# Tail groups worked one per period in periods 3 to 6, and layer 1 of group 7 computed with seven block products

## The chip, the cores and the metric

The kernel runs on one core of a Trainium2 chip. Its engines are TensorE (PE, with its weight loads shown apart as PEld), VectorE (DVE), ScalarE (ACT), GpSimd (POOL) and SyncE (SP), which issues nearly all DMAs. The metric is the device time of one execution in microseconds (us), as the median of several runs.

## The reference

```
# q, k, v: [8 batches, 8 heads, 576 positions, 64]
scores = q @ k.T / sqrt(64), kept where 0 <= pos_q - pos_k < 64, else -1e9
attn   = exp(scores - max) / (sum + 1e-9)
x      = attn @ v, heads side by side          # [8, 576, 512]
xn     = (x - mean) / sqrt(var + 1e-6) * g_ln
out    = x + max(xn @ w_ch1, 0) @ w_ch2        # 512 -> 2048 -> 512, float32
```

Each query sees itself and 63 earlier keys; then each row goes through a normalised two-layer network with a residual.

## The kernel before

The rows are worked in nine groups of 512. Groups 0 to 7 are the first 512 positions of batches 0 to 7. Group 8 (`NGRP - 1`, `r` in the main loop) gathers the last 64 positions of all batches: its four blocks of 128 rows are the four "tails", tail `i` holding batches `2i` and `2i + 1`. A block `(g, kb)` of any group passes these steps:

- scores on PE (`s_pe`, L352), exponentials on ACT (`s_exp`, L362), the mask on DVE (`s_mask`, L372);
- values product on PE (`b_pe`, L399); then on DVE `b_rows`: reciprocals of the row sums (L419), the division (L423), statistics (L429, L432);
- `z_step` on POOL: three small instructions and the normalised row in 16 bits (L451 to L457);
- `zt_step`: transposes z into `zT`, by a DMA transpose issued by SP (L477), or for some blocks by four PE transposes (L481) and a copy on ACT (L484).

The loads of a batch (L92, L179) are issued by SP, cast on POOL (L157, L185) and, for q and k, transposed by DMA (L268) or by PE (L279). `part_vB` (L204, L206) copies the cast v, shifted by 64 rows, by DMA. A tail is loaded by `load_tail` (six DMAs: tq, tk, tv, L106 and L109), cast by `cast_tail` on POOL (L118 to L121) and transposed by `t_tail`: tails 0 and 1 on PE (L301, L310), tails 2 and 3 by DMA (L297, L304).

The network is written in `mlp_units(g)`, a list of units. For groups 3 to 7 layer 1 is 16 units (`l1`, L504): four 128x512 matmuls each, and a ReLU on ACT (L508). Group 8 computes layer 1 with seven block products (Strassen's scheme in Winograd's form): each of four chunks `d` has the products 1, 2, 5, 6, 3, 7, 4 in `l1_a` to `l1_e`, four 128x256 matmuls each (L701). Their operands are sums of blocks of the weights (`w1_sums`, tiles `w1S`, L813, on DVE) and differences of blocks of zT (`z_sums`, L830, on DVE); ACT keeps copies of three of them (L713), DVE adds (L716) and takes maxima (L718, a third of them on POOL). Layer 2 of groups 1 to 8 is seven block products of two halves (`stage(n, p)`, L578), 14 units of eight matmuls, with the S sums of the hidden values before them (`s_sums`, L552) and the sums into the rows behind them (L587, L591), both on DVE. Groups 1 to 7 take the products in the order 4, 1, 2, 6, 5, 7, 3, group 8 in the order 1, 2, 6, 5, 7, 4, 3.

The main loop is the plan. Period `g` runs the units of group `g`, and after unit `i` everything that was put in slot `i` with `at(i, f, ...)`: the attention of group `g + 1` (`b` in the code), the loads of group `g + 3`, the casts and transposes of group `g + 2`, and the tails. An engine runs its instructions in the order written, so the slots are the order on every engine, and SP issues DMAs in that order too, each after its own waits. `TAILS = {3: [0], 5: [1], 7: [2, 3]}` says in which period a tail's attention is worked; its loads, casts and transposes lie in the period before. Period 7 also holds the W1 sums, and at its end the first products of group 8.

Of the kernel before, what the change touches and what calls it, by code (L numbers as in the profile page):

```python
# [18 lines left out]
def kernel(  # L19
# [77 lines left out]
    def load_tail(i):  # L97
        tq = p_in.tile([128, H, D], FP32, tag="tq32", name=f"tq32_{i}", bufs=1)
        tk = p_in.tile([128, 2, H, D], FP32, tag="tk32", name=f"tk32_{i}", bufs=1)
        tv = p_in.tile([128, 2, H, D], FP32, tag="tv32", name=f"tv32_{i}", bufs=1)  # L100
        tail32[i] = (tq, tk, tv)
        for n in range(6):
            r = n % 2
            b = 2 * i + r
            if n < 2:
                nc.sync.dma_start(out=tq[64 * r:64 * r + 64], in_=q[b, :, SM:S, :].rearrange("h s d -> s h d"))  # L106
            else:
                t, x = (tk, k) if n < 4 else (tv, v)
                nc.sync.dma_start(out=t[:, r], in_=x[b, :, S - 128:S, :].rearrange("h s d -> s h d"))  # L109
# [181 lines left out]
    def t_tail(i, x):  # L291
        src = tail16[i][x]
        if x == 0:
            tailT[i] = (p_qkt.tile([128, NHP, 128], FP16, tag="tqT", name=f"tqT_{i}", bufs=1),
                        p_qkt.tile([128, 2, NHP, 128], FP16, tag="tkT", name=f"tkT_{i}", bufs=1))
            if i >= 2:
                nc.sync.dma_start_transpose(out=tailT[i][0], in_=src[:, :, :].rearrange("p h d -> p (h d)"))  # L297
                return
# [3 lines left out]
        else:  # L302
            if i >= 2:
# [167 lines left out]
    def zt_step(g, kb, eng="act"):  # L471
# [4 lines left out]
        if XZ <= g and not ((kb == 3 and g in (2, 3, 5)) or (g, kb) == (3, 2)):  # L476
            nc.sync.dma_start_transpose(out=zT[g][:, :, 128 * kb:128 * kb + 128], in_=z)  # L477
            return
# [16 lines left out]
    def mlp_units(g, split=0, three=False, seven=True):  # L495
# [3 lines left out]
        units = []  # L499

# [55 lines left out]
        def product(n, p):  # L556
# [10 lines left out]
            if p == 0 and n in (1, 2 if last else 4, 5):  # L567
# [31 lines left out]
        def stage(n, p):  # L599
# [25 lines left out]
            elif n == 7:  # L625
                post_both("A", 2)
                store(2)
                store(3)
            elif n == 4:
                post("B", 2, 0)  # L630
                if last:
                    store_rest(2, slice(0, 256), None)
            elif n == 3:
# [41 lines left out]
        def l1_product(n, d):  # L675
# [12 lines left out]
            if n == 1:  # L688
                pool, tag = (ps_mm, "mm") if d == 2 else (ps_s, "sc")
                lbank[("A", d)] = pool.tile([128, 2, 256], FP32, tag=tag, name=f"lA_{d}")  # L690
            elif n == 2:
                lbank[("B", d)] = ps_t.tile([128, 2, 256], FP32, tag="t0", name=f"lB_{d}")
            elif n == 5:
                if d % 2:
                    lbank[("C", d)] = ps_t.tile([128, 2, 256], FP32, tag="t1", name=f"lC_{d}")
                else:
                    lbank[("C", d)] = ps_x.tile([128, 4, 256], FP32, tag="xps", name=f"lC_{d}")[:, 0:2]
# [85 lines left out]

        halves = [(half, i) for half in range(2) for i in range(split // 2)]
# [20 lines left out]
    def w1_sums(*which):  # L805
        wv = w1g[:, :, :].rearrange("p (a k) (i e m) -> p a k i e m", a=2, e=2, m=128)
        a11, a12, a21, a22 = (wv[:, b, :, :, a, :] for a, b in ((0, 0), (0, 1), (1, 0), (1, 1)))
        for n in which:
            w1S[n] = p_in.tile([128, NKC // 2, NHC // 2, 128], FP16, tag=f"qk32_{n % 2}", name=f"w1S{n}")
            o = w1S[n][:, :, :, :]  # L810
            x, y, op = {1: (a21, a22, ALU.add), 2: (w1S.get(1), a11, ALU.subtract),
                        3: (a11, a21, ALU.subtract), 4: (a12, w1S.get(2), ALU.subtract)}[n]
            nc.vector.tensor_tensor(out=o, in0=x, in1=y, op=op)  # L813
# [130 lines left out]
    def begin_last():  # L944
        nonlocal rest
        rest, _ = mlp_units(NGRP - 1)

    rest = None
    TAILS = {3: [0], 5: [1], 7: [2, 3]}
    for g in range(NGRP):  # L950
        if g == NGRP - 1:
            for _ in rest:
                pass
            break
        units, s_sums = mlp_units(g, (8, 16, 16)[g] if g < 3 else 0, g == 0, g > 0)
# [159 lines left out]
        elif g > 1 and b < B:  # L1115
            tail = TAILS.get(g)
# [6 lines left out]
            if tail:  # L1123
                r, i = NGRP - 1, tail[0]
                at(2, s_pe, r, i, False, "t")
                at(4, s_exp, r, i, 0)
                at(5, s_exp, r, i, 1)
                at(5, s_mask, r, i)
                at(7, b_pe, b, 1)
                at(7, b_pe, r, i, "t")  # L1130
                at(7, s_mm, b, 3)
                at(7, b_rows, b, 1)
                at(7, z_step, b, 1)
                at(8, s_mask, b, 3)
                at(8, b_rows, r, i)
                at(9, z_step, r, i)
                at(12, b_pe, b, 2)
                at(12, b_pe, b, 3, "sc")
                at(16, zt_step, r, i)
            else:  # L1140
                at(2, s_pe, b, 3, False, "t")
                at(4, s_exp, b, 3, 0)
                at(5, s_exp, b, 3, 1)
                at(5, s_mask, b, 3)
                at(7, b_pe, b, 1)
                at(7, b_pe, b, 2, "t")
                at(7, b_pe, b, 3, "sc")
                at(7, b_rows, b, 1)
                at(7, z_step, b, 1)
            if g + 2 < B:  # L1150
                at(5, alloc_qkT, g + 2)
                at(5, after_mask, *((NGRP - 1, tail[0]) if tail else (b, 3)))
# [3 lines left out]
            for j, i in ((2, 12), (3, 19)):  # L1156
                at(i, b_rows, b, j)
                at(i, z_step, b, j)
            for j in range(4):
                at((2, 14, 18, {3: 25, 5: 25}.get(b, 23))[j], zt_step, b, j)  # L1160
        for n, i in enumerate(TAILS.get(g, ()) if b >= B else ()):
            ts = (13, 13, 17, 22) if n else (1, 2, 5, 11)
            at(ts[0], s_mm, NGRP - 1, i)
            at(ts[1], s_mask, NGRP - 1, i)
            at(ts[2], b_step, NGRP - 1, i)
            at(ts[2], z_step, NGRP - 1, i)
            at(ts[3], zt_step, NGRP - 1, i)
        n = g + 2
        if g > 1 and n < B:
# [5 lines left out]
            at(26, part_vB, n, 0, 4)  # L1175
# [12 lines left out]
        if g > 2:  # L1188
# [60 lines left out]
```

## Time and profile before

Three runs took 299.7 to 299.91 us, median 299.87. The profiled execution took 299.59 us, of which 297.9 us are the span from its first to its last instruction.

| stretch of the span, us | what | PE busy | DVE busy | ACT busy | POOL busy |
|---|---|---|---|---|---|
| 0 to 48.7 | start, period 0's first part | 45.95 | 27.61 | 27.76 | 36.70 |
| 119.4 to 150.16 | period 3, tail 0 worked | 30.76 | 23.64 | 17.37 | 18.98 |
| 150.16 to 180.96 | period 4, tail 1 loaded and transposed | 30.80 | 22.16 | 16.59 | 18.13 |
| 180.96 to 211.76 | period 5, tail 1 worked | 30.80 | 23.63 | 17.37 | 18.75 |
| 211.76 to 240.09 | period 6, tail 2 loaded and transposed | 28.33 | 20.24 | 11.42 | 12.59 |
| 240.09 to 268.3 | period 7, tails 2 and 3 worked | 28.21 | 20.81 | 11.89 | 7.91 |
| 268.3 to 297.9 | rest of group 8, last stores | 25.08 | 22.35 | 8.62 | 6.06 |

How to read the views that follow: in the windows view a line is a stretch, then for each engine its busy time and the count of instructions. In the timeline a line is start, length, engine, line of the kernel, operation, tiles written and read, and in brackets the idle time before it with the instruction that ended it. The chain of work that ended last gives start, length and engine. A line such as L578 is that of the kernel before.

### The profile page before, as it was taken

How to read it: one execution, taken by the hardware profiler on the slowest of the kernel's cores; microseconds unless marked ns; L12 is line 12 of the kernel's file. 1: busy time of each engine (PE TensorE's matmuls, PEld its weight loads, DVE VectorE, ACT ScalarE, POOL GpSimd, SP SyncE). 2: the span in 40 equal slices, each digit the busy share in tenths (PEclk: the TensorE clock that was granted, in tenths of full speed). 3: DMA queues.
4: the chain of work that ended last, by engine and by line, in shares of the span. 5: the costliest groups of instructions: out<-in, count | busy, mean ns of one | idle time of the engine just before them, and what ended most of it. 6: DMA issues, size and time to landing. Idle time of an engine off the chain costs nothing.

```text
span 297.9 us, 7824 instructions
## 1 busy us (share of the span) xinstructions
PE 290.6 (98%) x3187; PEld 206.9 (69%) x3187; DVE 217.9 (73%) x414; ACT 154.4 (52%) x261; POOL 164.2 (55%) x243
## 2 busy tenths in 40 slices
PE   8989999999999999999999999999999999999994
PEld 3657545888888888557854786469646854788883
DVE  2881378899993894489757865698568786789983
ACT  3566647677449526873276428751674056305500
POOL 4688897753850986389518860897048407024300
PEclk9999999999999999999999999999999999999998
DMA  7999999979979999998299999991729497003014
GB/s 189 259 382 339 382 296 284 256 217 300 170 169 302 248 155 223 291 229 143 55 303 257 184 179 274 291 162 40 223 47 183 72 178 194 20 18 143 2 37 107
DMA packets 113223, 58.11 MB, mean 195 GB/s; under 512 B 82593, under 2 KB 104161, under 8 KB 113186
## 3 DMA queue, kind: packets, MB, share of 16 engines
q1 hardware_dynamic: 112752, 57.21, 81.7%
q8 instruction: 25, 0.41, 0.6%
q10 hardware_dynamic: 434, 0.40, 0.4%
q14 instruction: 12, 0.10, 0.1%
HBM read 38.80 MB, written 9.44 MB: 162 GB/s over the span
## 4 chain that ended last, share of the span: by engine, by line
PE 83%; DMA 6%; SPq 5%; POOL 3%; issue 0%; DVE 0%
PE hps L504 24%; PE pA L578 14%; PE hph L645 10%; PE pB L578 10%; PE pC L578 9%; PE xps L399 3%; DMA w2s<-in_moe_w_ch_dram 3%; PE sc L352 3%; DMA wT<-in_moe_w_ch_dram 3%; PE lA L701 2%; PE tp L279 2%; SPq L179 2%; POOL w2s L246 2%; SPq L218 2%; SPq L87 1%; PE lC L701 1%
## 5 line engine op out<-in xcount | busy, mean ns | idle before, releaser
L504 PE MATMUL hps<-zT,w1g 128*128 128x512 f16 x352 | 80.2, 379 | 0.0
L508 ACT ACTIVATE hrT<-hps 128x512 f16<-128x512 f32 x88 | 52.8, 600 | 36.8 <-PE hps L504 33.8
L504 PEld LDWEIGHTS <-w1g 128*128 128x128 f16 x352 | 33.1, 98 | 38.0 <-issue 1.7
L578 PEld LDWEIGHTS <-sS 128*128 128x128 f16 x512 | 49.3, 98 | 5.6
L362 ACT ACTIVATE pt<-sc 128x512 f16<-128x512 f32 x72 | 39.8, 601 | 22.7 <-PE sc L352 22.2
L451 POOL TENSOR_SCALAR rsz<-mvg 128x1 f32<-128x1 f32 x32 | 10.5, 329 | 63.2 <-DVE mvg L432 53.2
L578 PEld LDWEIGHTS <-hrT 128*128 128x128 f16 x384 | 36.7, 98 | 7.0 <-ACT hrT L508 0.8
L645 PE MATMUL hph<-zT,w1g 128*128 128x256 f16 x320 | 37.9, 273 | 0.0
L372 DVE TENSOR_TENSOR pt<-pt,mask 128x1024 f16<-128x1024 f16 x32 | 23.5, 740 | 19.6 <-ACT pt L362 19.6
L157 POOL CAST qk<-qk 128x1024 f16<-128x1024 f32 x29 | 32.5, 1139 | 8.9 <-PE sc L352 5.9
L645 PEld LDWEIGHTS <-w1g 128*128 128x128 f16 x320 | 30.4, 98 | 4.5 <-POOL w1g L233 0.2
L578 PE MATMUL pC<-w2s,sS 128*128 128x256 f16 x256 | 31.2, 273 | 0.0
L578 PE MATMUL pA<-wT,sS 128*128 128x256 f16 x256 | 30.9, 273 | 0.0
L650 ACT ACTIVATE hrT<-hph 128x512 f16<-128x512 f32 x40 | 24.1, 605 | 10.8 <-PE hph L645 10.6
L260 ACT COPY qkT<-tp 128x1024 f16<-128x1024 f16 (+1 forms) x18 | 17.3, 962 | 23.2 <-PE tp L279 21.3
L552 DVE TENSOR_TENSOR sS<-hrT 128x1024 f16<-128x1024 f16 (+2 forms) x41 | 26.3, 641 | 2.0 <-ACT hrT L508 1.9
L423 DVE TENSOR_TENSOR xn<-xps,rcp 128x256 f32<-128x256 f32 (+1 forms) x50 | 25.8, 538 | 1.8 <-DMA out_dram<-xn 1.1
L429 DVE BATCH_NORM_STATS2 stats<-xn 128x6 f32<-128x512 f32 x36 | 25.0, 694 | 1.2
L457 POOL TENSOR_SCALAR z<-xn,rsz 128x512 f16<-128x512 f32 x24 | 22.4, 932 | 2.5
L452 POOL TENSOR_TENSOR rsz<-rsz,mhalf 128x1 f32<-128x1 f32 x32 | 20.6, 643 | 2.7
L185 POOL CAST vA<-v 128x1024 f16<-128x1024 f32 (+1 forms) x18 | 16.7, 943 | 4.2 <-DMA v<-in_v_dram 3.9
L399 PEld LDWEIGHTS <-pt 128*64 128x64 f16 x576 | 11.4, 110 | 9.1 <-issue 4.3
(120 smaller groups left out, 422.6 us busy)
## 6 DMA issues: line engine op xcount, KB each, us to landing
qk<-in_q_dram SPq DMA_DIRECT2D x16, 512.0 KB, 6.1
qk<-in_k_dram SPq DMA_DIRECT2D x16, 512.0 KB, 7.2
out_dram<-xn SPq DMA_DIRECT2D x32, 256.0 KB, 3.5
v<-in_v_dram SPq DMA_DIRECT2D x28, 256.0 KB, 7.5
w2s<-in_moe_w_ch_dram SPq DMA_DIRECT2D x9, 512.0 KB, 8.5
w1s<-in_moe_w_ch_dram SPq DMA_DIRECT2D x4, 512.0 KB, 7.2
tk<-in_k_dram SPq DMA_DIRECT2D x8, 256.0 KB, 4.8
tv<-in_v_dram SPq DMA_DIRECT2D x8, 256.0 KB, 5.4
```

The source lines that it names most:

```text
L157: nc.gpsimd.tensor_copy(out=dst[:, :].rearrange("p (a j) e d -> p a e j d", j=j), in_=t[:, :].rearrange("p (a e j d) -> p a e j d", e=2, j ...
L362: nc.scalar.activation(out=o, in_=i, func=AF.Exp, bias=0.0, scale=scale)
L372: nc.vector.tensor_tensor(out=ptv, in0=ptv, in1=mb, op=ALU.mult)
L423: nc.vector.tensor_tensor(out=xn[:, n * i:n * i + n], in0=xps[:, :, 0:D], in1=rcp_b, op=ALU.mult)
L429: nc.vector.bn_stats(out=stats, in_=xv)
L457: nc.gpsimd.tensor_scalar(out=z, in0=xv, scalar1=rs, scalar2=nm, op0=ALU.mult, op1=ALU.add)
L504: nc.tensor.matmul(out=hps, lhsT=w1g[:, kc, 128 * hc:128 * (hc + 1)], rhs=zT[g][:, kc, :], start=(kc == 0), stop=(kc == NKC - 1),)
L508: nc.scalar.activation(out=hrT[:, hc, :], in_=hps, func=AF.Relu, bias=0.0, scale=1.0)
L552: nc.vector.tensor_tensor(out=o, in0=x, in1=y, op=op)
L578: nc.tensor.matmul(out=o, lhsT=a[:, c, 128 * p:128 * p + 128], rhs=wv[:, c, :], start=(first and (p == 0 or split_c) and c == 0), stop=(c ...
L645: nc.tensor.matmul(out=hps[:, e], lhsT=w1g[:, kc, 128 * hc:128 * (hc + 1)], rhs=zT[g][:, kc, 256 * half:256 * half + 256], start=(kc == 0) ...
L650: nc.scalar.activation(out=hrT[:, 2 * i:2 * i + 2, 256 * half:256 * half + 256], in_=hps, func=AF.Relu, bias=0.0, scale=1.0)
```

## The change

- Tails are worked one per period: tail `g - 3` in periods 3 to 6. In each of these periods the block handled at the early slots (2 to 9) is `x` and the one at the later slots (7 to 19) is `y`: the tail and block (b, 3), in period 6 the other way round. `TAILS` goes.
- `load_tail` is in two parts, q and k apart from v, at other slots; the cast of tail 3 is in period 5's slot 27. Tail 0 is transposed by DMA; only tail 1 is left to PE.
- `zt_step`: block 3 of groups 4 and 6 is transposed by PE in place of DMA. With them groups 2 to 6 do so, now at slot 26.
- `part_vB` stands at slot 22 (period 3) or 20 (4 and 5) in place of 26.
- `w1_sums` takes a part of the tile and is called in periods 5 and 6.
- Group 7 (`mixed`, as group 8): layer 1 by seven block products, group 8's order of layer 2 products and S sums. Its z differences and first products stand at the end of period 6; the tiles of the differences serve both groups.

```
-            if i >= 2:
+            if i != 1:
                 nc.sync.dma_start_transpose(out=tailT[i][0], in_=src[:, :, :].rearrange("p h d -> p (h d)"))
...
-        if XZ <= g and not ((kb == 3 and g in (2, 3, 5)) or (g, kb) == (3, 2)):
+        if XZ <= g and not ((kb == 3 and g < 7) or (g, kb) == (3, 2)):
...
+        mixed = g >= NGRP - 2
...
             elif n == 7:
                 post_both("A", 2)
-                store(2)
-                store(3)
+                if not mixed:
+                    store(2)
+                    store(3)
             elif n == 4:
                 post("B", 2, 0)
                 if last:
                     store_rest(2, slice(0, 256), None)
+                elif mixed:
+                    store(2)
+                    store(3)
...
+        if mixed:
+            def with_sums(f, a, c0, n):
+                f(*a)
+                s_sums(c0, c0 + 4, n)
+
+            units = [lambda: l1_b(0)]
+            for d in range(1, 4):
+                units += [lambda d=d: l1_a(d), lambda d=d: l1_c(d - 1), lambda d=d: l1_b(d), lambda d=d: l1_e(d - 1)]
+            units[8] = lambda: with_sums(l1_e, (1,), 0, 1)
+            units += [
+                lambda: with_sums(stage, (1, 0), 0, 2), lambda: with_sums(l1_c, (3,), 4, 1),
+                lambda: stage(1, 1), lambda: with_sums(l1_e, (3,), 4, 2),
+                lambda: stage(2, 0), lambda: stage(2, 1),
+            ]
+            for n, m in ((6, 3), (5, 4)):
+                for p in range(2):
+                    units.append(lambda n=n, m=m, p=p: with_sums(stage, (n, p), 4 * p, m))
+            for n in (7, 4, 3):
+                for p in range(2):
+                    units.append(lambda n=n, p=p: stage(n, p))
+            l1_a1(0)
+            return units, lambda: l1_a2(0)
...
-    def w1_sums(*which):
+    def w1_sums(n, ks=(0, 1)):
...
+        k = slice(ks[0], ks[-1] + 1)
+        nc.vector.tensor_tensor(out=w1S[n][:, k], in0=x[:, k], in1=y[:, k], op=op)
...
-    TAILS = {3: [0], 5: [1], 7: [2, 3]}
+    begun = {}
+
+    def begin(g):
+        begun[g] = mlp_units(g)
...
+            r, i = NGRP - 1, g - 3
+            x, y = ((r, i), (b, 3)) if g < 6 else ((b, 3), (r, i))
...
+            at(2, s_pe, *x, False, "t")
...
+            at(7, b_pe, b, 1)
+            at(7, b_pe, *x, "t")
+            at(7, s_mm, *y)
...
+            at(8, s_mask, *y)
+            at(8, b_rows, *x)
+            at(9, z_step, *x)
+            at(12, b_pe, b, 2)
+            at(12, b_pe, *y, "sc")
...
+            at(12, b_rows, b, 2)
+            at(12, z_step, b, 2)
+            at(19, b_rows, *y)
+            at(19, z_step, *y)
+            at(2, zt_step, b, 0)
+            at(14, zt_step, b, 1)
+            at(29 if g == 4 else 16 if g < 6 else 25, zt_step, r, i)
+            at(18, zt_step, b, 2)
+            at(26 if g < 6 else 16, zt_step, b, 3)
...
-            at(26, part_vB, n, 0, 4)
+            at({3: 22, 4: 20, 5: 20}.get(g, 26), part_vB, n, 0, 4)
...
+        if 2 <= g < 6:
+            i = g - 2
+            at((15, 18, 4, 18)[i], load_tail, i, "qk")
+            at((15, 23, 4, 21)[i], load_tail, i, "v")
+            at(24 if i < 3 else 27, cast_tail, i)
+            at((26, 27, 26, 30)[i], t_tail, i, 0)
+            at((26, 29, 26, 30)[i], t_tail, i, 1)
+        if g == 5:
+            at(23, w1_sums, 3, (0,))
+            at(25, w1_sums, 1)
+        if g == 6:
+            at(0, w1_sums, 2)
+            at(3, w1_sums, 4)
+            at(3, w1_sums, 3, (1,))
+        if g in (6, 7):
+            i = 25 if g == 6 else 23
+            at(i, z_sums, g + 1, 1, 2)
+            at(i + 2, z_sums, g + 1, 3, 4)
+            at(i + 3, begin, g + 1)
+            at(i + 4, (lambda: begun[7][1]()) if g == 6 else (lambda: next(begun[8][0])))
```

## The prediction

> **What bounds the kernel now.** I read the page's busy times first, then the same figures cut into the kernel's periods, then the chain that ended last, and only then the queues of VectorE (DVE), GpSimd (POOL) and SyncE (SP) around the places that the change touches.
>
> ```profile
> PE 290.6 (98%) x3187; PEld 206.9 (69%) x3187; DVE 217.9 (73%) x414; ACT 154.4 (52%) x261; POOL 164.2 (55%) x243
> PEclk9999999999999999999999999999999999999998
> 119.40:150.16 30.76, 30.76 (x354) 20.56 (x352) 23.64 (x48) 17.37 (x29) 18.98 (x28) 1.00 0.86 183
> 150.16:180.96 30.80, 30.80 (x338) 20.90 (x336) 22.16 (x44) 16.59 (x29) 18.13 (x27) 1.00 1.17 232
> 211.76:240.09 28.33, 28.33 (x274) 18.65 (x272) 20.24 (x42) 11.42 (x21) 12.59 (x20) 1.00 0.60 123
> 240.09:268.30 28.21, 28.21 (x242) 18.01 (x240) 20.81 (x35) 11.89 (x21) 7.91 (x12) 1.00 0.49 103
> ```
>
> The four last lines are periods 3, 4, 6 and 7: start and end, length, then busy time of PE, PEld, DVE, ACT and POOL, the granted clock, DMA share and GB/s. In each of them TensorE (PE) is busy for the whole length at full clock, so the end of the kernel moves by what PE's own instructions lose or gain, plus any wait that PE has to make. All other engines have room: DVE, the fullest, 4.5 to 8 us in each period. The chain view says what PE's instructions cost when they follow each other:
>
> ```profile
> 246.24 7.01 PE hps L504 x32
> 273.17 0.94 PE lA L701 x8
> 282.72 0.66 PE pB L578 x6
> 283.38 0.03 issue
> 283.41 1.27 PE pB L578 x10
> 284.68 1.75 PE pA L578 x16
> ```
>
> 32 wide matmuls (128x512) take 7.01 us, 219.1 ns each; 80 narrow ones (128x256) stand in the chain from 229.62 to 238.35, 109.1 ns each. A PE transpose costs 0.45/8 = 56 ns. The mean durations in the page's groups (379 and 273 ns) overlap and are not used.
>
> **The change, part by part.**
>
> *Layer 1 of group 7.* Removed: 64 wide matmuls, 64 x 219.1 = 14.02 us. Added: 7 products x 4 chunks x 4 = 112 narrow ones, 112 x 109.1 = 12.22 us. All of it is PE time on the path: **-1.80 us**. ACT's count stays (16 copies or ReLUs of 128x512 for 16 ReLUs). DVE gets 12 sums at 0.69 and 8 maxima at 0.29, 10.6 us, and four z differences, 2.1 us; POOL four maxima at 1.5 us, in a stretch where it has nothing else.
>
> A rule that speaks against it: the Trainium skill (TensorE: Matmul & The Clock Gate, Back-to-back issue gap) gives a sustained spacing of about 81 ns for 128 columns and about 131 ns for 512. By an estimate halfway between, 98 ns for 256, the blocks would cost 11.0 us against 8.4, a loss of 2.6 us in place of a gain. The trace disagrees: 219.1 and 109.1 ns, a half for half the columns.
>
> *Waits inside that layer.* Group 8 already runs it. From 266.54 to 284.68, 18.14 us, it holds 112 narrow matmuls of L701 and 48 of L578: 160 x 109.1 = 17.46. So PE loses 0.68 us there, on DVE sums and ACT copies that have only just ended (the pB split at 283.38 is one). DVE is busy 16.77 of these 18.14 us. Group 7 gets the same order of products; its start is easier, since z differences 1 and 2 are placed before the stage (7) sum and not after it. I take **+0.6**; ends 0.3 (only the late split) and 1.0 (half as much again).
>
> *Transposes on PE.* Tail 0's 12 go to the DMA queue, z(4,3)'s and z(6,3)'s 8 come to PE: -4 x 0.056 = **-0.22 us**.
>
> *Tails moved.* Periods 4 and 6 get a tail each that period 7 loses two of. In period 7 layer 1, 96 layer 2 products and two tails take 26.45 us up to 266.54; less 14.02 and 10.47 that leaves 1.96, 0.98 a tail. Period 3 (with a tail) is 30.76; period 4 without one is 30.80 including 16 PE transposes (0.90) that period 3 lacks, so a tail costs 0.86 there. **-0.2** for two; ends -0.4 and +0.3.
>
> *DVE's new places.* In period 6 W1 sums 2 (1.23 us), 4 (1.47) and half of 3 (0.7) enter a queue that stands thus now:
>
> ```profile
> 212.41 0.68 DVE L372 TENSOR_TENSOR pt<-pt,mask 128x1024 f16<-128x1024 f16 x1
> 214.80 0.21 DVE L419 RECIPROCAL rcp<-xps 128x8 f32<-128x8 f32 x1 [1.72 <-PE xps L399]
> 216.60 0.66 DVE L372 TENSOR_TENSOR pt<-pt,mask 128x1024 f16<-128x1024 f16 x1
> 219.30 0.69 DVE L372 TENSOR_TENSOR pt<-pt,mask 128x1024 f16<-128x1024 f16 x1 [2.05 <-ACT pt L362]
> ```
>
> The bracket is the idle time before the line and what ended it. Sum 2 falls in the 1.72 us, sums 4 and 3 (2.2) in the 2.05: the mask at 219.30 is late by some 0.15. That mask is block (7,3)'s, whose values product now comes second on PE, near 220.2 (period 3's order), with the mask done at 220.1: a margin of 0.1, and a wait of 0.1 or 0.2 us if POOL slows the sums. It is counted in the +0.2 below. In period 5 half of sum 3 and sum 1 (1.9 together) fall into idle stretches of 0.59, 1.05 and 0.23 us after 207: the next mask is some 0.2 late, with over 2 us to the product that reads it. Period 6 then has DVE full (20.2 + 2.5 tail + 3.4 + 1.9 differences = 28 of 29.2), but the S sums of periods 3 and 5, in the same order, end 2 us before their products, which is the margin here too. 0 on the path for the rest; without that cover the price is the lateness, one for one.
>
> *New waits for transfers.* Four: (a) tail 0's DMA transposes stand on SP behind the vB copies that end at 115.7; with 1.4 to 1.85 us and 1.25 us of issue and 3.2 us to landing, the second lands near 121, and PE reads it near 122. The four output stores queued behind move from 117.6-120.6 to about 121.0, so the loads of group 5 start 0.45 us later; their casts start at 127.85. (b) Tail 2's transposes in period 4 wait on POOL's casts and hold SP until about 30.2 us into the period; the stores and the loads for group 7 behind them go 1.5 us later than now, and the third cast of group 7 ends 0.3 us later. (c) Tail 3's transposes follow the stores after period 5 and land about 2 us before their scores. (d) Tail 1 is loaded at slot 18 of period 3 and not at slot 4 of period 4, behind z(4,2)'s transpose on SP (issued 141.36 to 142.55). Its q lands near 147 and is cast by 146.6 to 147.8, against PE's transpose at 148.5; its k is issued at 144.6 and lands, at 3.1 to 5.4 us, between 147.7 and 150.0, is cast 1.04 us later, and PE wants it at 150.6. That is 0 to 0.5 us late. The DMA row has a light slice there (2 tenths, 55 GB/s). The vB copies, moved from slot 26 to 20 or 22, still wait on SP for the v casts (143.3), and tail 1's v behind them is cast near 152, before POOL's next work at 155.5. I take **+0.2** for all of these; ends 0 and 1.5 (q and k both at the slow end and one engine step behind).
>
> *z(b,3) on PE.* In periods 3 and 5 the transpose after unit 26 replaces a DMA after unit 23. In the queue of POOL:
>
> ```profile
> 143.39 0.23 POOL L451 TENSOR_SCALAR rsz<-mvg 128x1 f32<-128x1 f32 x1
> 143.71 0.61 POOL L452 TENSOR_TENSOR rsz<-rsz,mhalf 128x1 f32<-128x1 f32 x1
> 144.41 0.56 POOL L453 TENSOR_SCALAR rsz<-mvg,rsz 128x1 f32<-128x1 f32 x1
> 145.08 0.77 POOL L457 TENSOR_SCALAR z<-xn,rsz 128x512 f16<-128x512 f32 x1
> ```
>
> z(4,3) is there at 145.85; unit 26 ends at 146.87 (half of the pA stretch from 145.99). Slack 1.0 us; in period 5 207.44 against 208.46, 1.0, less the 0.3 of (b). The new tail casts stand behind these z, not before them. 0 on the path; from 1.0 us lateness on, PE stands.
>
> Sum: -1.80 + 0.6 - 0.22 - 0.2 + 0.2 = **-1.42 us**. The profiled execution took 299.59 us (span 297.9 and 1.69 around it), so 298.17; the median of the runs, 299.87, is 0.28 above it: **298.4**. With all low ends -2.1 (297.8), with all high ends +0.8 (300.7).
>
> **Rivals.**
>
> 1. *POOL is late for z(b,3) (slower).* In periods 3 to 5 POOL runs without a pause from the q and k casts to this z; one z there took 2.17 us in place of 0.77 while DVE ran S sums. Another such stretch (1.4) with 0.3 of late loads makes 1.7, and PE would stand 0.7 us at the transpose in each of three periods: +2.1, **300.6**. It decides from 1.7 us late on. For: POOL has no gaps there. Against: the order ahead of this z is the one that period 3 has now, 2.17 included.
> 2. *Tail 1 comes late to PE.* A wait of 1 to 1.5 us replaces my 0.2: **299.3 to 299.8**. For: margins under 1 us; against: the light DMA slice.
> 3. *The block layer is paced by DVE*, so that the change does not do what it says: DVE 92% busy in group 8's stretch; if leftovers of period 6 keep it 1.5 us behind, the gain is gone: **299.9**. Against: its queue into group 8 was as full, and cost 0.68.
> 4. *Narrow matmuls cost more than half.* Break-even is 14.02/112 = 125 ns. At three quarters of a wide one, 164 ns, layer 1 would cost 18.4 us, +4.4, and with the other terms **304.6**. Every stretch of this trace has 109, so next to nothing is left for it. The two spacings of the Trainium skill above stand in that proportion (98 to 131).
>
> **How the numbers follow.** My forecast 0.68 (297.6 to 299.2); rival 1 0.12; rival 2 0.09, a third of it still faster; rival 3 0.07; rival 4 0.01; a stall that I have not seen 0.03. A difference of 0.2%, 0.6 us, is about what a measurement can tell: faster 0.71, same 0.14, slower 0.15. The range, 297.6 to 300.5, leaves out the larger half of rival 1, rival 4, the unseen and a little below.
>
> **What would show it.** Right: PE's work between group 6's last product and group 8's first L701 (pieces that reach into period 6 counted with it) shorter by about 3.2 us, periods 3, 4, 5 and 6 longer by 0.9, 0.2, 0.2 and 0.9, period 2 shorter by 0.7; no wait of PE over 0.5 us. Wrong: a wait of PE's transposes for POOL (z or the tail's casts) or, in the chain, DMA of tail loads; gaps between the L701 pieces ended by DVE sums totalling over 1.5 us.

## The result and the profile after

The changed kernel takes **305.0 us**, the median of four runs (303.94 to 306.39), against 299.84 for the kernel before on the same chip: a ratio of 1.0165, 95% interval 1.0146 to 1.0185. The forecast was 298.4, its range 297.6 to 300.5. The profiled execution took 304.8 us, its span 303.1. One execution of a later run, `t0_on_pe`, was in a slow state at 751.29 us and is in no figure below.

The page of the kernel after, the rows that answer to those shown of before:

```profile
PE 290.1 (96%) x3231; PEld 211.3 (70%) x3231; DVE 230.8 (76%) x435; ACT 153.8 (51%) x261; POOL 171.3 (57%) x247
...
PEclk9999999999999999999999999999999999999999
DMA  8999999959989999999999999997991121003014
```

PE has 0.5 us less work than before and the clock is full, yet the span is 5.2 us longer: PE stands. The windows view of periods 3 to 6 (start and end, length, busy time of PE, PEld, DVE, ACT and POOL, clock, DMA share, GB/s) says where:

```profile
118.72:152.37 33.65, 31.98 (x370) 21.33 (x367) 26.82 (x50) 17.56 (x31) 21.66 (x31) 1.00 1.04 215
152.37:185.44 33.07, 31.46 (x360) 20.81 (x358) 23.64 (x47) 17.96 (x30) 22.36 (x32) 1.00 1.07 224
185.44:216.95 31.51, 31.13 (x357) 20.76 (x356) 26.67 (x50) 17.07 (x30) 19.91 (x30) 1.00 1.02 218
216.95:247.85 30.90, 29.33 (x306) 19.32 (x305) 26.04 (x54) 12.74 (x23) 15.31 (x22) 1.00 0.45 88
```

Every period has idle PE now; before, none had. What PE waited for, and below it what DVE waited for (total, times, longest):

```profile
PE xps L400 <- DVE pt L373: 1.6, 1, 1.6
PE pB L580 <- DVE xn L593: 1.3, 2, 0.6
...
PE ztp L482 <- POOL z L458: 1.0, 1, 1.0
PE tpk L311 <- POOL tk L121: 0.8, 1, 0.8
...
PE pA L580 <- DVE xn L593: 0.4, 1, 0.4
```

```profile
DVE xn L424 <- DMA out_dram<-xn: 7.4, 5, 2.2
```

The waits of PE shown here have four releasers on two engines, which looks like many small mishaps. They have a queue in common: POOL's z stood 2.0 us for a transpose that had not landed and its cast of tk 2.3 us for the load, and both are issued by SP. For the waits on DVE, its one line leads there too: the division L424 (L423 before, where it waited 1.1 us in all) writes into the `xn` buffer of an earlier group, and that buffer's output store has not landed. DVE's timeline at the start of period 6 shows it go through to PE (start, length, operation; in brackets the idle time before and what ended it):

```profile
219.97 0.21 DVE L420 RECIPROCAL rcp<-xps 128x8 f32<-128x8 f32 x1 [0.33 <-PE xps L400]
222.37 0.69 DVE L424 TENSOR_TENSOR xn<-xps,rcp 128x512 f32<-128x512 f32 x1 [2.19 <-DMA out_dram<-xn]
...
223.92 0.66 DVE L373 TENSOR_TENSOR pt<-pt,mask 128x1024 f16<-128x1024 f16 x1
224.50 1.22 DVE L842 TENSOR_TENSOR w1S<-w1g,w1S 128x2048 f16<-128x2048 f16 x1
225.63 0.68 DVE L842 TENSOR_TENSOR w1S<-w1g 128x1024 f16<-128x1024 f16 x1
226.23 0.69 DVE L373 TENSOR_TENSOR pt<-pt,mask 128x1024 f16<-128x1024 f16 x1
```

```profile
226.97 0.22 PE L400 MATMUL xps<-vB,pt 128*64 128x65 f16 x1 [1.57 <-DVE pt L373]
```

The idle time that the W1 sums were to fill is spent waiting for the store; the sums then run back to back, the mask of block (7,3) behind them ends at 226.92, and PE stands 1.57 us. And the stores are late mainly because SP issues them late: the second of the four, for which that division stood by the landing times, was issued 1.6 us into period 6 and landed in 3.9 us; before, it was issued 0.6 us ahead of the period's start and landed in 2.9. SP's queue in period 4 (152.4 to 185.4; start, time that the issues took, line, tiles, count):

```profile
157.23 5.51 SPq L180 DMA_DIRECT2D v<-in_v_dram  x2
162.90 3.42 SPq L478 DMA_TRANSPOSE zT<-z  x1
166.37 1.20 SPq L180 DMA_DIRECT2D v<-in_v_dram  x2
167.61 1.69 SPq L108 DMA_DIRECT2D tq<-in_q_dram  x2
169.34 1.45 SPq L110 DMA_DIRECT2D tk<-in_k_dram  x2
170.84 2.62 SPq L102 DMA_DIRECT2D tv<-in_v_dram  x2
173.56 4.74 SPq L269 DMA_TRANSPOSE qkT<-qk  x2
178.40 2.55 SPq L478 DMA_TRANSPOSE zT<-z  x2
```

There is hardly a free moment in it. The four stores begin at 185.40, 33.0 us into the period; before, they began 29.2 us into it. How full is the queue? A line of the timeline can join issues that lie apart. In period 5 before, one line is

```profile
198.66 10.00 SPq L477 DMA_TRANSPOSE zT<-z  x4
```

but each of these four issues takes 1.2 us; in the other 5.2 us SP stands between them, nearly all of it until POOL has the next z. So the table adds up the single issues (from the start to the end of each, the waits between them left out), beside the length of the period (both from one period's first L504 or L506 matmul to the next one's):

| length / SP issuing, us | period 3 | period 4 | period 5 |
|---|---|---|---|
| before | 30.74 / 22.2 | 30.79 / 27.0 | 30.81 / 23.4 |
| after | 33.81 / 31.0 | 32.90 / 31.2 | 31.50 / 28.7 |

### The profile page after: what moved, and what is told of

Same layout as the page of the kernel before. It is cut to its first block, busy times and chain, and to the rows that moved or that the text cites. A ratio compares the mean times of both kernels' runs of the same rounds, so it can differ in the third digit from the quotient of the medians.

```text
span 303.1 us, 7975 instructions
## 1 busy us (share of the span) xinstructions
PE 290.1 (96%) x3231; PEld 211.3 (70%) x3231; DVE 230.8 (76%) x435; ACT 153.8 (51%) x261; POOL 171.3 (57%) x247
## 3 DMA queue, kind: packets, MB, share of 16 engines
q1 hardware_dynamic: 113264, 57.34, 80.7%
## 4 chain that ended last, share of the span: by engine, by line
PE 60%; DVE 14%; DMA 9%; POOL 7%; SPq 4%; issue 3%; ACT 1%; POOLq 0%; DVEq 0%; ACTq 0%
PE hph L651 10%; PE pA L580 9%; PE hps L506 8%; PE pC L580 7%; PE pB L580 5%; PE lA L707 4%; DVE sS L554 4%; PE ch L668 4%; DMA qk<-in_q_dram 3%; DVE xn L424 3%; DVE stats L430 3%; PE sc L353 3%; PE xps L400 2%; DMA qk<-in_k_dram 2%; PE lC L707 2%
## 5 line engine op out<-in xcount | busy, mean ns | idle before, releaser
L506 PE MATMUL hps<-zT,w1g 128*128 128x512 f16 x288 | 65.9, 379 | 0.0
L510 ACT ACTIVATE hrT<-hps 128x512 f16<-128x512 f32 x72 | 43.2, 600 | 20.7 <-PE hps L506 17.0
L506 PEld LDWEIGHTS <-w1g 128*128 128x128 f16 x288 | 27.0, 98 | 30.7 <-issue 1.5
L373 DVE TENSOR_TENSOR pt<-pt,mask 128x1024 f16<-128x1024 f16 x32 | 27.1, 856 | 10.1 <-ACT pt L363 10.1
L651 PEld LDWEIGHTS <-w1g 128*128 128x128 f16 x320 | 30.4, 98 | 4.5
L424 DVE TENSOR_TENSOR xn<-xps,rcp 128x256 f32<-128x256 f32 (+1 forms) x50 | 25.8, 539 | 8.0 <-DMA out_dram<-xn 7.4
L580 PE MATMUL pA<-wT,sS 128*128 128x256 f16 x256 | 31.4, 273 | 0.4 <-DVE xn L593 0.4
L580 PE MATMUL pC<-w2s,sS 128*128 128x256 f16 x256 | 31.4, 273 | 0.0
L452 POOL TENSOR_SCALAR rsz<-mvg 128x1 f32<-128x1 f32 x32 | 9.8, 307 | 37.8 <-DVE mvg L433 35.4
L724 POOL TENSOR_SCALAR hrT<-hrT 128x512 f16<-128x512 f16 x8 | 11.9, 1488 | 29.4 <-DVE hrT L722 29.4
L453 POOL TENSOR_TENSOR rsz<-rsz,mhalf 128x1 f32<-128x1 f32 x32 | 21.6, 674 | 2.7
L400 PEld LDWEIGHTS <-pt 128*64 128x64 f16 x576 | 11.5, 110 | 11.5 <-issue 5.8
```

What stands on the lines that cost most here:

```text
L373: nc.vector.tensor_tensor(out=ptv, in0=ptv, in1=mb, op=ALU.mult)
L424: nc.vector.tensor_tensor(out=xn[:, n * i:n * i + n], in0=xps[:, :, 0:D], in1=rcp_b, op=ALU.mult)
L506: nc.tensor.matmul(out=hps, lhsT=w1g[:, kc, 128 * hc:128 * (hc + 1)], rhs=zT[g][:, kc, :], start=(kc == 0), stop=(kc == NKC - 1),)
L510: nc.scalar.activation(out=hrT[:, hc, :], in_=hps, func=AF.Relu, bias=0.0, scale=1.0)
L580: nc.tensor.matmul(out=o, lhsT=a[:, c, 128 * p:128 * p + 128], rhs=wv[:, c, :], start=(first and (p == 0 or split_c) and c == 0), stop=(c ...
L651: nc.tensor.matmul(out=hps[:, e], lhsT=w1g[:, kc, 128 * hc:128 * (hc + 1)], rhs=zT[g][:, kc, 256 * half:256 * half + 256], start=(kc == 0) ...
```

## Experiments

The theory after this reading, Q: SP's queue is overfilled by the tails' loads and transposes, which now come in four periods running; stores and transposes go out late, and DVE, POOL and PE pay. The rivals, V: DVE has too much to do since the block layer and the W1 sums came; P: POOL's casts are too many and too late.

### The tails' plan alone, and three ways to relieve it

`tails_only`: the tails as in the change; layer 1 of group 7, its S sums and the W1 sums as before.

```
-        mixed = g >= NGRP - 2
+        mixed = g >= NGRP - 1
...
-        if 2 < g < NGRP - 2:          # S sums
+        if g > 2:
```

> The changed kernel's plan for the tails, loads and transposes in periods 3 to 6, but group 7 and the W1 sums as in the kernel before (16 wide units, sums in period 7). Theory Q (SP's queue: more DMAs in periods 3 to 5 than it can issue, so output stores are late, VectorE's division waits for them and everything behind it is late for PE): the loss is in the tails' plan, periods 3 and 4 stay near 33.6 and 33.1 us, and the time is 299.84 - 0.5 (PE's own instructions) + about 5 (waits) = 304.4. Rival V (the block layer and the W1 sums overload VectorE, and the loss comes with them): periods 3 and 4 fall back to 31.6 and 31.0, time 299.4 to 300.

Measured: **304.33 us**, ratio 1.0162 (1.0098 to 1.0227). All of the loss is there without the block layer, so V falls as the main cause. The next three tried to take single weights off.

`t0_on_pe` (tail 0 transposed by PE, as before: `if i >= 2` for `if i != 1` in `t_tail`):

> The changed kernel with tail 0 transposed by PE again in period 2, so that SP has no two DMA transposes ahead of the output stores there. Theory Q: VectorE's wait of 1.74 us for the stores at the start of period 3 falls under 0.3, PE's wait of 0.63 us for the sum after product 4 in period 3 goes, PE pays 0.67 us more for 12 transposes; total -0.1 to -0.4, so 304.7. Rival V: the 0.63 us stays, total +0.6, 305.6.

`w1_late` (W1 sums 2, 4 and the half of 3 in period 6's slots 8, 19 and 20 for 0 and 3):

> The changed kernel with the three W1 sums of period 6 moved from slots 0 and 3 to slots 8, 19 and 20, behind the mask of block (7,3). Theory Q with these sums as the second half: the late stores (2.19 us of VectorE's wait) and the two sums of 1.9 us together make PE's wait of 1.57 us for the mask; without the sums the mask ends near 225.3 where PE asks at 225.4, so the wait goes to under 0.3 and the time to 303.6. If the late stores alone make it: no change, 305. In both cases the waits in periods 3 and 4 stay.

`loads_on_act` (the tails' 24 loads issued from ScalarE's queue, `nc.scalar.dma_start`):

> The changed kernel with the tails' 24 loads issued by ScalarE's queue and not by SyncE's, in the same slots. Theory Q: SP gets 24 issues fewer (13 to 17 us of its time over periods 2 to 5), VectorE's waits for stores (1.74, 1.46, 0.97, 2.19) fall under 0.5 each, POOL's wait of 1.96 us for a z buffer in period 4 goes; PE's waits of some 5.5 us fall under 2, against about 0.6 us of ScalarE per issue: 300.5 to 302. Rival V or a rival P (GpSimd's load): no gain over 1 us, 304 or more.

Measured: **308.01** (305.19 to 308.62; ratio 1.0233, 1.0171 to 1.0295), **305.23** (1.0197, 1.0133 to 1.0262) and **316.5** (1.055, 1.0509 to 1.0591). None helped, and the first is slower than either theory expected. In it the division of period 6 waited 3.5 us for a store and PE 3.0 for the mask behind it: the chain shown above, longer, and behind it came a stretch at half clock (see `more_loads_before` below). In the second PE's wait for that mask fell from 1.6 to 0.4 us, but the division still waited 2.8 us and PE stood 1.9 us for a sum into the rows later in the period: moving the sums moves the debt. The third shows why a queue on a working engine is dear. The waits view of ACT in that run:

```profile
ACT qkT L261 <- DMA tk<-in_k_dram: 9.4, 1, 9.4
ACT hrT L510 <- DMA tk<-in_k_dram: 9.2, 1, 9.2
```

Twice ACT came to the six loads of a tail, which had to wait to be issued, and its ReLUs and copies behind them stood for more than 9 us. The Trainium skill (Perfetto Trace Analysis, DMA Optimizations) says that balancing DMAs over the engines that can issue them may help where descriptor generation is the limit. Here it cost 11.5 us, since an engine's instructions stand behind the issue.

### Is it the loads, their number, or their packets?

`loads_left_out`: tails 1 to 3 are not loaded. `more_loads_before`: the kernel before with extra loads in periods 3 and 5 and nothing else.

```
     def load_tail(i, part):
+        if i > 0:
+            tail32[i] = tail32["kept"]      # tail 0's tiles
+            return
```

```
+        if g in (3, 5):                     # in the kernel before
+            at(18, load_tail, (g - 1) // 2, 0, 4)
+            at(21, load_tail, (g - 1) // 2, 4, 6)
```

> The changed kernel without the loads of tails 1 to 3 (18 transfers, six each in periods 3, 4 and 5): the casts take tail 0's numbers again, so the part of the output that belongs to the later tails is that of wrong inputs; everything behind the loads is still done. Theory Q (SP's queue is full, stores go out late, the division waits for them): the six issues cost SP 4.1 us in period 3 and 5.8 in period 4, the stores go out that much earlier, the waits of the division fall from 7.4 to about 2 us in all, and periods 3 and 4 go from 33.65 and 33.07 to about 31.3 each: 299.5 to 301.5. Rival V (VectorE has too much work): its work is the same, 304.5 to 305. Rival P (GpSimd's casts too late and too many): the casts no longer wait for the loads (tq 1.4, tk 2.3, tv 4.1 us), the same number of them runs: 302.5 to 304.

> The kernel before with the change's extra load and nothing else of it: in periods 3 and 5, which load no tail, tail 1's and tail 2's six loads are made once more than needed, at slots 18 and 21; nothing reads them before the real load comes in the next period. No engine has more work, only SP's queue and the DMA. Theory Q: SP was busy for 28.7 and 28.8 us of these 30.8 us periods and gets 4 to 5 us more, so stores and transposes slip 2 to 3 us and each period grows by 0.7 to 2 us: 301.3 to 304. Rivals V and P: 299.9 to 300.2.

Measured: **299.14 us** (ratio 0.9968, 0.9954 to 0.9982) and **308.28** (1.0252, 1.0209 to 1.0294). Eighteen loads out of the changed kernel are worth 5.9 us; twelve more in the kernel before cost 8.4, more than foreseen. In the latter, periods 3 and 5 grow to 34.02 and 33.67 us with SP issuing for 30.5 and 30.1; no engine has more to do, and PE waits for things that SP issues:

```profile
PE hps L507 <- DMA zT<-z: 3.1, 1, 3.1
PE hps L507 <- DMA tv<-in_v_dram: 2.7, 1, 2.7
```

Both are the first matmul of a period, which reads zT. The second line names tv by inference; the last transpose of z, issued behind the extra loads, landed at 220.02 and the matmul began at 220.11. The division waited only 0.8 us here. So the loads alone bring a loss of this kind, though in this kernel by way of a late transpose and not of late stores, and without them the changed kernel has none; P falls too.

Part of the 8.4 us is PE's clock. The clock row of this run's page, and the windows line of its period 4:

```profile
PEclk9999999999999999999979999999999999999998
154.08:186.44 32.36, 32.36 (x337) 21.32 (x338) 20.51 (x42) 16.57 (x28) 18.20 (x27) 0.95 1.15 230
```

As the wait of 3.1 us ends, the granted clock is a half for 3.4 us. PE is busy for the whole of period 4, which is 1.6 us longer than before at a mean clock of 0.95. The profiled execution of the changed kernel, where no such wait of PE is longer than 1.6 us, has the full clock.

Next, which property of the loads. `fewer_issues_after` joins two stores into one and a tail's two loads of k, and of v, into one each; `fewer_issues_before` joins the stores of the kernel before:

```
-                store(2)
-                store(3)
+                store_two(2)                # out[g, 256:512] in one transfer
...
-        for r in range(2):
-            nc.sync.dma_start(out=tk[:, r], in_=k[2 * i + r, :, S - 128:S, :].rearrange("h s d -> s h d"))
+        nc.sync.dma_start(out=tk, in_=k[2 * i:2 * i + 2, :, S - 128:S, :].rearrange("r h s d -> s r h d"))
```

> The changed kernel with the same bytes in fewer transfers: two output stores of 256 rows for four of 128 in each group, and one load each for a tail's k and v for two (four transfers for six). Theory Q, if an issue costs SP by the transfer (0.55 to 0.7 us where nothing holds it): four issues or 2.5 us fewer in a period, about half of what the tails added, 301.5 to 303.5. Theory Q, if SP's time goes by the bytes or by landings: 304.5 to 305.5. Rivals V and P: 304.5 to 305.

> The kernel before with two output stores for four in each group. Its SP queue has 2 to 3 us free in each of periods 3 to 5 and its division waits for stores only 1.1 us in all, so theory Q expects little: 299.3 to 300.0. V and P: 299.9. More than 0.5 us below 299.9 would say that the queue held up the kernel before too.

`large_packets` keeps number and bytes of the loads and makes their rows 2 KB long:

```
+    def rows(x, b, n):
+        return x[b].rearrange("h s d -> (h s d)")[0:512 * n].rearrange("(p m) -> p m", m=512)
```

> The changed kernel with as many tail loads of as many bytes, each from one contiguous stretch of q, k or v: rows of 2 KB for rows of 256 bytes, so an eighth of the packets. It reads other numbers than it should, so the tails' part of the output is wrong; the work behind the loads is the same. Leaving 18 loads out took the queue's packet time from 80.7% of 303.1 us to 74.3% of 297.6 us, 23.5 us or 7.8 us for a tail of 1.31 MB, 168 GB/s, where the page's slices show up to 387 GB/s. If the DMA engines' time is what is short (theory Qd), 2 KB rows should cost about half, 4 us less in a period: 299.5 to 302. If it is the number of transfers that SP issues and waits for (theory Qi): 304.3 to 305.2.

Measured: **304.22 us** (1.0134, 1.0079 to 1.019), **299.94** (0.9996, 0.9985 to 1.0008), **299.32** (0.9983, 0.9971 to 0.9995). Four of some 27 transfers a period fewer bring 0.8 us, within the scatter of that kernel's runs (302.81 to 306.17); the same transfers with an eighth of the packets bring 5.7, nearly as much as no loads at all. It is the time of the packets, then, and not the count of the issues that matters (the longer rows also lie one behind the other in memory, which this run does not separate). SP's queue in period 4 of `large_packets`, for the last six of the lines shown above:

```profile
162.17 2.35 SPq L183 DMA_DIRECT2D v<-in_v_dram  x2
164.57 1.27 SPq L111 DMA_DIRECT2D tq<-in_q_dram  x2
165.89 1.06 SPq L113 DMA_DIRECT2D tk<-in_k_dram  x2
166.99 0.90 SPq L105 DMA_DIRECT2D tv<-in_v_dram  x2
167.99 4.42 SPq L272 DMA_TRANSPOSE qkT<-qk  x2
172.51 3.35 SPq L481 DMA_TRANSPOSE zT<-z  x2
```

The six loads hold SP for 3.23 us in place of 5.76, and the stores begin at 181.27, 30.0 us into the period. In packet time (the page's share of the queue times the span): the change has 80.7% of 303.1 = 244.6 us, without the 18 loads 74.3% of 297.6 = 221.1, so 7.8 us a tail; with 2 KB rows 78.2% of 297.7 = 232.8, so 3.0 us less for each of the four tails, 4.9. In both differences the packets of other transfers may have become quicker too. The Trainium skill (DMA: Bandwidth & Descriptors, Why small descriptors are slow) gives trn2 about 3 cycles on top of 8 for a 256-byte packet and 32 bytes of descriptor for each. By an estimate from that, with the descriptor taken as one more cycle, 2 KB rows need 68 cycles for 96, 0.71 of the time. The runs show 4.9 for 7.8, 0.62, so the trace agrees roughly.

`copies_on_act` keeps the joined transfers and takes others off the queue: the shifted copy vB of groups 5 to 7, two transfers of 455 KB together in a period, is made by ScalarE after layer 1, where it has little to do (the edit on top of the joined transfers):

```
-            at({3: 22, 4: 20, 5: 20}.get(g, 26), part_vB, n, 0, 4)
+            if g > 2:
+                for j, i in enumerate((22, 23, 24, 25)):
+                    at(i, copy_vB, n, j)    # nc.scalar.copy, 64 partitions
```

> The changed kernel with the merged stores and loads of the earlier run (304.2), and the shifted copy vB of the v tiles of groups 5 to 7 made by four ScalarE copies at slots 22 to 25, where ScalarE has little to do, in place of two transfers of 455 KB together in periods 3, 4 and 5 each. Output as the reference's. Qd: 455 KB at 170 to 230 GB/s are 2 to 2.7 us of the DMA engines in each period, about a third of a tail's load; the 6 us that the tails cost fall by 2 to 4: 300 to 302. Qi: two of some 24 transfers fewer in a period, as much as two of the four merged ones brought, 0.4: 303.5 to 304. Against both: ScalarE's four copies take some 4 us and could hold up the evacuations of zT, +0 to 1.

Measured: **299.87 us** (1.0003, 0.999 to 1.0016), 4.3 below `fewer_issues_after`. More than a third of a tail's load should have given: the loss is steep once the queue is full, and small again as soon as it is not. Whether it was the copies' transfer time or their two places in the queue is not separated here.

### What is left: the block layer and a repaired version

`tails_loads_left_out` is `tails_only` without the loads:

> The earlier run with the tails' plan alone (layer 1 of group 7 and the W1 sums as before, 304.3), without the loads of tails 1 to 3, as in the run of the changed kernel that took 299.14; the later tails' output is that of wrong inputs. It stands against that run as the block layer and the W1 sums in their new places do, without the crowded queue. By the prediction (layer 1 -1.80, waits inside it +0.6, PE's transposes the same): 300.2 to 300.6. If the block layer gives nothing, as 305.0 against 304.3 has it with the loads: 298.5 to 299.3.

Measured: **299.92 us** (1.0012, 0.9991 to 1.0033), 0.8 above the same with the block layer. Then three runs to get the rest back: vB's copies on ScalarE in period 2 too; besides, tail 1's loads at slots 13 and 18 for 18 and 23; besides, four z buffers for three.

> The earlier run with merged transfers and vB's copies on ScalarE (299.87), with the same for group 4, in period 2: two transfers of 455 KB less ahead of tail 0's transposes and of group 2's stores. If the DMA's backlog from period 2 is what makes PE wait for tkT (0.3 us there) and the division wait for stores in period 3 (2.4 us): both fall, 299.2 to 299.7. If period 2's end was free: 299.8 to 300.0; if ScalarE's copies hold up period 2's evacuations: 300.2.

> The run just above with tail 1's loads of q and k at slot 13 for 18 and of v at slot 18 for 23 in period 3, so ahead of the three zT transposes. If the late load is what PE waits for (tpk behind tk's cast, 0.5 us, and pB's bank): another 0.3 to 0.6 us off, 298.8 to 299.4. If the time only goes over to the transposes behind them (z's buffers): no change or +0.5.

> The run just above with four buffers for z instead of three (g1 lies in tq32's buffer to make room), so that GpSimd's z does not wait for a transpose that SP issues late (0.9 us in period 4 in the earlier run). If this wait reaches PE: 0.2 to 0.5 below the run above; else the same.

Measured: **303.91**, **304.83** and **302.5 us** (1.0139, 1.0124 to 1.0155; 1.0162, 1.0149 to 1.0175; 1.0084, 1.0062 to 1.0105): all slower, by an edit that went wrong. ScalarE's timeline in period 2 of the first:

```profile
114.41 1.06 ACT L211 COPY vB<-vA 64x1040 f16<-64x1040 f16 x1 [5.55 <-POOL vA L184]
115.49 1.01 ACT L268 COPY qkT<-tp 128x1024 f16<-128x1024 f16 x1
```

The copy stood 5.55 us for POOL's cast of v, the evacuation of qkT stood behind it, and PE waited 3.1 us, with half the clock for 3.4 us behind that. But in periods 3 to 6 of the third run the waits view lists no wait of PE. So `repaired` leaves period 2 as the change has it and keeps the rest; `repaired_p2` also has period 2's copies on ScalarE, behind the evacuations. A part of the edit of `repaired`:

```
-            at((15, 18, 4, 18)[i], load_tail, i, "qk")
-            at((15, 23, 4, 21)[i], load_tail, i, "v")
+            at((15, 13, 4, 18)[i], load_tail, i, "qk")
+            at((15, 18, 4, 21)[i], load_tail, i, "v")
...
+        z = p_blk.tile([128, DM], FP16, tag="z", name=f"z_{g}_{kb}", bufs=4)
```

> The run with merged transfers and vB's copies on ScalarE in periods 3 to 5 (299.87), with tail 1's q and k loaded at slot 13 for 18 and its v at slot 18 for 23, and four z buffers for three. Period 2 is the changed kernel's. The last run's periods 3 to 6 were 31.18, 31.41, 30.97 and 30.03 us against 31.97, 32.07, 30.95 and 30.49 in the 299.87 run, 1.9 us less; taken from 299.87: 298.0 to 298.8, if the slow period 2 in front of them did not give them that (a delay there lets the DMA catch up); then 299.2 to 299.9.

> The run just above with period 2's two vB transfers also made by ScalarE, at slots 26 and 28, behind the evacuations of qkT and zT that the copies held up before. If tail 0's transposes and the stores behind period 2's transfers still cost something: 0.2 to 0.6 below the run above. If ScalarE's copies hold up the exponentials at slot 28: 0.3 to 1 above it.

Measured: **299.01 us** (0.9968, 0.9955 to 0.998) and **299.37** (0.9977, 0.9965 to 0.9989). The first is faster than both kernels by more than its interval. Its page and PE's waits over 0.3 us (the warm-up of PE apart):

```profile
PE 289.4 (97%) x3231; PEld 211.6 (71%) x3231; DVE 228.8 (77%) x435; ACT 164.6 (55%) x273; POOL 171.0 (58%) x247
```

```profile
PE ztp L489 <- DVE z L451: 0.6, 1, 0.6
PE xps L407 <- ACT pt L370: 0.5, 2, 0.3
```

The division's waits for stores are down from 7.4 to 1.5 us. Is the gain the change's or the repairs'? `repaired_before` gives the kernel before the same repairs, `repaired_tails_only` gives them to `tails_only`:

> The kernel before with the same repairs (merged stores and tail loads, vB's copies of groups 5 to 7 on ScalarE, four z buffers), and nothing of the change; its plan has no tail 1 load in period 3 to move. If the gain of the repaired kernel (299.01) is the change's: PE waited for almost nothing in the kernel before, 299.6 to 300.0. If it is the repairs': 299.0 to 299.3.

> The tails' plan alone (group 7's layer 1 and the W1 sums as before), with all of the repairs, tail 1's earlier load too. Against 299.01 it stands as the block layer does: 299.8 by the difference of the two runs with the loads left out (0.8), 300.2 by the prediction (1.2).

Measured: **299.9 us** (0.9993, 0.9978 to 1.0008) and **299.82** (0.9998, 0.9987 to 1.0009). The repairs do nothing for the kernel before; the tails' plan, repaired, is worth nothing measurable; the block layer is worth 0.8.

| length / SP issuing, us | period 3 | period 4 | period 5 | median |
|---|---|---|---|---|
| more loads, before | 34.02 / 30.5 | 32.36 / 26.5 | 33.67 / 30.1 | 308.3 |
| tails only | 33.73 / 31.8 | 32.64 / 30.7 | 31.26 / 28.7 | 304.3 |
| fewer issues, after | 33.35 / 31.2 | 31.78 / 30.1 | 31.06 / 27.0 | 304.2 |
| copies on ACT | 33.08 / 26.6 | 30.96 / 27.6 | 30.95 / 27.7 | 299.9 |
| large packets | 32.37 / 26.6 | 30.96 / 27.3 | 30.96 / 26.1 | 299.3 |
| repaired | 32.06 / 26.4 | 30.96 / 28.5 | 31.04 / 26.1 | 299.0 |

In this table and the one above, periods 4 and 5 of the kernels with tails in every period take 30.95 to 31.06 us where SP issues for up to 28.5 us, 31.26 and 31.50 at 28.7, and 31.78 to 32.90 from 30.1 on. Period 5 with more loads fits (33.67 with 30.1); its period 4 owes its length to the clock, as shown. The queue is not the only thing that costs: in `copies_on_act_p2` and `copies_and_early_tail1`, with three z buffers, periods 4 and 5 take 31.4 to 31.9 us with 27.2 to 28.1 of issues, and why is not settled; with the fourth buffer they take 30.96. Period 3 varies by up to 1 us besides, with tail 0's transposes and tail 1's k (PE waited 0.8 us for tkT in `loads_left_out`, 0.5 for tk's cast in `copies_on_act`).

## Why the prediction was wrong

Differences to the kernel before, in us, as the prediction forecast them, after, and in the repaired kernel (the last row from the end of period 6 to the end of the span; the prediction's sum of -1.42 holds 0.2 more for new waits that it gave to no period):

| | forecast | after | repaired |
|---|---|---|---|
| up to the end of period 2 | -0.7 | -0.7 | -0.3 |
| period 3 | +0.9 | +3.1 | +1.3 |
| period 4 | +0.2 | +2.1 | +0.2 |
| period 5 | +0.2 | +0.7 | +0.2 |
| period 6 | +0.9 | +2.6 | +0.8 |
| from there to the end | -3.2 | -2.6 | -3.1 |

- **The step that failed is "New waits for transfers", +0.2 with ends 0 and 1.5.** It measured about 6: 305.0 against 299.14 without the loads. The prediction followed each moved transfer from its issue to its reader and compared two times at each place; it had tail 1's k "0 to 0.5 us late" (0.8), and stores 1.5 us late in period 4. The stores of period 4 came not 1.5 us later in the period but 3.9 (33.0 us into it for 29.2). What it did not do was add up the queue. Before, SP issued for 22.2, 27.0 and 23.4 us in periods 3, 4 and 5, and the loads of a tail took 5.8 us of that in period 4. With them in periods 3 and 5, a transpose of z (1.2) fewer there, and tail 2's two transposes (2.8) more in period 4, an estimate from these rows is 26.8, 29.8 and 28.0: period 4 is past the 28.5 us up to which the runs above lost little, and period 5 comes near it. Measured were 31.0, 31.2 and 28.7. Such a sum would have warned of the loss but not given its size: stores slip over into the next period, and single issues grow (the first of the four stores behind period 3 from 0.36 to 2.51 us). It also took a light slice of the DMA row (55 GB/s) as room; in the row of after no slice of periods 3 to 5 is light. Periods with and without a tail's load alternated before, with DMA shares of 0.86 and 1.17 in the prediction's lines of periods 3 and 4; after, periods 3 to 5 all have 1.02 or more.
- **What the stores feed was not asked.** The prediction had the stores 0.4 and 1.5 us later, and followed what stands behind them on SP, the next loads. Their other reader, the division that writes into the stored buffer again, is not in it. That wait grew from 1.1 to 7.4 us; in period 6 it carried the delay to the mask and to PE, as shown. For the sums of layer 2 the same is likely but was not followed.
- **Covers that were gone.** "0 on the path for the rest" for DVE's new places named idle stretches as cover; the stores took them. The mask of (7,3), counted 0.1 to 0.2 late, was 1.6 late. z on PE with a slack of 1.0 came 1.0 late in period 4, as POOL waited 1.96 us for a z buffer that a late transpose still read. And a margin was overlooked: layer 2's second product takes the bank of the fourth; PE waited 0.6 us for it in periods 3 and 4, and once more with large packets.
- **The rivals.** Rival 2 had the right mechanism at one place and a fraction of its size; rival 1's place (z in period 4) had the wait, with another cause. Rivals 3 and 4 did not come: the block layer's stretch and its narrow matmuls, 0.44 us for four or 109 ns each in the chain of after, are as forecast.
- **What was right.** With the queue relieved the periods come out as forecast within 0.1 us, but for period 3, 0.4 longer, and the end of period 2. The block layer with its waits, forecast at -1.2, measures -0.8 in both pairs (299.92 to 299.14, 299.82 to 299.01), a third less by the medians; the ratios to before differ by 0.0044 and 0.0030, 1.3 and 0.9 us, so 1.2 is not excluded. The tails' plan, forecast at -0.42 with its transposes and +0.2 for waits, measures -0.1 with the repairs (299.82 to 299.9), nothing beyond the scatter.
- **A slip in the working.** DVE's room was given as 4.5 to 8 us in each period; by the lines shown it is 7.1 to 8.6. Nothing in the sum hung on it.

## What to carry to other kernels

When transfers are moved in a kernel bound by its matmul engine, add up the single issues of the queue by period before following single transfers, and leave out the time in which the queue itself waits. Here periods of 31 us lost little with up to 28.5 us of issues and more from 28.7 on, and what a full queue delays is everything behind, not only what was added. For each output store ask who writes its buffer next; for each idle stretch used as cover ask what ends it and whether the change moves that. And where loads have rows of 256 bytes, the rows are dearer than the number of transfers: fewer packets, or other transfers taken off the queue, gave back here what joining issues did not.

## What the hardware showed that was not expected

- The time that SP needs for an issue depends on what else is under way: two loads of tv took 2.62 us in the crowded queue and 0.90 with 2 KB rows at the same place, and two loads of 256 KB of v took 5.51 us at one place and 1.20 at another.
- The loads of a tail issued from ScalarE held ScalarE's own instructions for 9.4 us.
- A long wait of PE costs more than it lasts. In the traces of these runs (the start apart), the granted clock was a half for 3.4 us behind six of the seven waits of PE of 2.5 to 3.1 us, and for 10.2 us behind one of 9.3; behind those of 2.0 us or less it stayed full. 3.4 us at half clock are 1.7 us of PE's work. The slowest of the four runs of the changed kernel, 306.39 us, has a mean clock of 0.994 where the others have 0.998 or 0.999; it has no trace.
- The DMA share is no measure of room by itself: the repaired kernel has shares of 1.13 and 1.14 in periods 3 and 4 with hardly a wait, the changed one 1.04 and 1.07 with many. The time of SP's issues told the two apart, 26.4 and 28.5 us against 31.0 and 31.2.
